# Preparing two dense weight units instead of one beside the experts, and a weight ring of six buffers instead of eight

## The chip, the cores and the metric

The kernel runs on one core of one Trainium2 chip. The metric is device time in microseconds (us) of one execution, as the median of several runs. The engines are named as in the profile: PE multiplies matrices (PEld is its weight load), DVE and ACT are the vector and the scalar engine, POOL is GpSimd, SP only issues DMA transfers.

## The reference, cut to what matters

```
attn_out = banded attention(q, k, v)               # 2 x 8 heads, 576 tokens, window 64
x = attn_out as (1152, 512)
logits = x @ w_gate;  expert = argmax(logits)      # 8 experts
h = np.maximum(einsum('ecd,edf->ecf', disp, w1), 0.0)   # w1: 8 x 512 x 1024, float32
y = einsum('ecf,efd->ecd', h, w2)                  # w2: 8 x 1024 x 512, float32
out[i] = gate_w[i] * y[expert of i, place of i]
h = out @ w_in                                     # dense layer, 512 x 2048, float64 weights
g = h * np.clip(h + 3.0, 0.0, 6.0) / 6.0
return (g @ w_out).astype(np.float32)              # 2048 x 512, float64 weights
```

## The kernel before, in words

The first 75 us are attention and routing. After them come the experts and then the dense layer, and this case is about the weights of these two parts.

**Units and pieces.** The weights are cut into 40 *units* of 256 hidden columns: units 0 to 31 are the eight experts' four quarters each, units 32 to 39 are the dense layer's. A unit has two halves (0: the up-projection, 1: the down-projection), and a half two *pieces* of 128x512 numbers, so a unit has pieces 0 to 3. Every matrix product is done in three passes on a pair of tiles, a rounded part and a remainder (`PASSES`), so before PE can use a piece, it must be *split*: a copy on ACT (L253, the rounded part) and a subtraction on DVE (L258, the remainder), into a tile called `wt`. The experts of two small slots skip the split and multiply from the raw tile.

**Dense pieces cost more.** Their weights arrive as 64-bit numbers and are *converted* first: two instructions on ACT (L201, L204) and four on DVE (L208, L212, L217, L224), in `conv64`. The conversion writes back into the raw tile; for one dense unit it writes into four tiles of its own, `first_w0` to `first_w3`, where the converted piece waits unsplit.

**Buffers.** Raw tiles come from a ring of 8 buffers (`rawp`, `r_raw`); the split halves from a ring of `2 * NWT` = 8 buffers (`wp`, `r_wt`), taken in the order of the units.

**Steps.** PE's work is a list of 84 steps written out in `ORDER` and `GROUPS`: steps 0 to 43 are the experts (three teams, of 16, 12 and 16 steps), steps 44 to 51 the first 640 tokens against dense units 32 to 35 (two steps to a unit), 52 to 67 the other 512 tokens against units 32 to 39, then the rest. Step 20 is the first that uses unit 15; step 44 is the first of the dense part. In a step PE makes the up-projection, in a later one the down-projection of the same slice.

**The planner.** Loads, conversions and splits are *jobs*, each with a due number, sorted by it. While the program is written, an estimate of each engine's clock is kept (`est`); after each group of matmuls `fill` issues the jobs that the estimate has room for, and `need` forces those without which the next step can't run. So the order of instructions on ACT, DVE and SP's queue is settled when the program is built, and each engine then keeps to it. A load gets its place in the raw ring from a count (`raw_at`), the split half its place from `wt_at`.

**The unit that is prepared early.** For unit 32 (`dense0`) the table `FIRST_AT = (5, 9, 14, 20)` says beside which unit each of its four pieces is loaded and converted, into `first_w`. Its splits, and all work on units 33 to 39, have due numbers near their own unit's, that is at the end of the experts and in the dense part.

Of the kernel before, what the change touches and what calls it, by code (L numbers as in the profile page):

```python
# [10 lines left out]
F32R = mybir.dt.float32r  # L11
# [12 lines left out]
def tile_kernel(ctx, tc, q, k, v, w_gate, w1, w2, w_in, w_out, out, cap):  # L24
# [159 lines left out]
    def conv64(u, i, dst=None):  # L184

        box = {}

        def load():
            box["raw"] = raw = rawp.tile([128, 2 * HW], F32, name="raw").bitcast(U32)
            if i < 2:  # L190
                src = w_in32[256 * i : 256 * i + 256, 2 * FU * u : 2 * FU * u + 2 * FU]
                nc.sync.dma_start(raw.rearrange("p (c f) -> p c f", c=2), src.rearrange("(c p) f -> p c f", p=128))
            else:
                r0 = FU * u + 128 * (i - 2)
                nc.sync.dma_start(raw, w_out32[r0 : r0 + 128, :])
            w = raw.rearrange("p (n t) -> p n t", t=2)
            box["lo"], box["hi"] = w[:, :, 0], w[:, :, 1]

        def c_abs():
            box["c"] = cv.tile([128, HW], U32, name="c64")  # L200
            nc.scalar.activation(box["c"].bitcast(F32), box["hi"].bitcast(F32), AF.Abs)  # L201

        def c_round():
            nc.scalar.activation(box["lo"], box["lo"], AF.Copy, scale=2.0 ** -29)  # L204

        def c_clamp():
            c = box["c"].bitcast(F32)
            nc.vector.tensor_scalar(out=c, in0=c, scalar1=TINY, scalar2=HUGE, op0=ALU.max, op1=ALU.min)  # L208

        def c_shift():  # L210
            c = box["c"]
            nc.vector.tensor_scalar(  # L212
                out=c, in0=c, scalar1=0x07FFFFFF, scalar2=3, op0=ALU.bitwise_and, op1=ALU.logical_shift_left
            )

        def a_join():
            nc.vector.scalar_tensor_tensor(  # L217
                out=box["c"], in0=box["hi"], scalar=0xC0000000, in1=box["c"],
                op0=ALU.bitwise_and, op1=ALU.bitwise_or,
            )  # L220

        def t_add():
            out = box["lo"] if dst is None else dst.bitcast(U32)
            nc.vector.tensor_tensor(out=out, in0=box["c"], in1=box["lo"], op=ALU.add)  # L224

        return box, (load, c_abs, c_round, c_clamp, c_shift, a_join, t_add)

    NC64 = 2
# [5 lines left out]
    HALF = UW // 2  # L234
# [12 lines left out]
    def split_ops(w, r, i):  # L247
        n = HALF // 2
        hi, lo = w[:, 0, n * i : n * i + n], w[:, 1, n * i : n * i + n]

        def high(e):
            if e == "A":
                nc.scalar.copy(hi, r)  # L253
            else:
                V.tensor_copy(hi, r)

        def low():
            V.tensor_tensor(out=lo, in0=r, in1=hi.bitcast(F32), op=ALU.subtract)  # L258

        return high, low  # L260
# [28 lines left out]
    key, rank = (rt.tile([128, E], F32, name=n) for n in ("key", "rank"))  # L289
# [720 lines left out]

    NWT = 4
    NRAW = 8
    FIRST_AT = (5, 9, 14, 20)
    NPC = 4
    EOFF = (mybir.EngineType.Activation, mybir.EngineType.DVE)
    NDS = DFF // 128
# [3 lines left out]
    LATE, BESIDE = 10, 2  # L1020

    rawp = ctx.enter_context(tc.tile_pool(name="rawp", bufs=NRAW))
    wp = ctx.enter_context(tc.tile_pool(name="wp", bufs=2 * NWT))
    wk_ctx = ExitStack()
    wk = wk_ctx.enter_context(tc.tile_pool(name="wk", bufs=2))

# [3 lines left out]
    units, steps, unit_of = [], [], {}  # L1030
# [10 lines left out]
    for n, (small, b) in enumerate(TEAMS):  # L1041
        at_ = dict.fromkeys("abw", 0)
# [22 lines left out]
    est = dict.fromkeys(("PE", "A", "V", "P", "D"), 0.0)  # L1065
# [18 lines left out]
            self.rel.append(None)  # L1084
            return len(self.rel) - 1

    r_raw, r_wt, r_ct = Ring(NRAW), Ring(2 * NWT), Ring(NC64)

    def whole(m):

        kind, s, _ = units[m]
        return kind == "e" and SCAP[s] == 64

    wt_at, raw_at = {}, {}
    dense0 = unit_of["d", 0, 0]
    for m in range(len(units)):
        if m != dense0:
            for n in range(2 if units[m][0] == "e" else NPC):
                raw_at[m, n] = len(raw_at)
            for i in range(NPC):  # L1100
                if FIRST_AT[i] == m:
                    raw_at[dense0, i] = len(raw_at)
        for h in range(2):
            if not whole(m):
                wt_at[m, h] = len(wt_at)
    raw_t, raw_ready, wt, half_ready, pieces = {}, {}, {}, {}, {}
    e_of = {}
# [6 lines left out]
    def load_job(m, h):  # L1114
        _, s, u = units[m]

        def gate():
            return r_raw.free(raw_at[m, h])

        def run(e, fin):  # L1120
            take_raw(m, h)
            if u == 0:
                e_of[s] = expert(s)
            weights_in(raw_t[m, h], e_of[s], u, h)
            raw_ready[m, 2 * h] = raw_ready[m, 2 * h + 1] = fin + 3.5
            if whole(m):
                half_ready[m, h] = fin + 3.5
            return fin

        return [({"D": 1.46}, gate, run)]  # L1130

    def conv_job(m, i):
        u = units[m][2]
        ix = {}
        first = m == dense0
        b, (load, c_abs, c_round, *mid, t_add) = conv64(u, i, first_w[i] if first else None)

        def run_load(e, fin):
            r_raw.take()
            load()  # L1140
            raw_t[m, i] = first_w[i] if first else b["lo"].bitcast(F32)
            return fin + 3.5

        def run_abs(e, fin):
            ix["ct"] = r_ct.take()
            c_abs()
            return fin

        def plain(fn):
            def run(e, fin):  # L1150
                fn()
                return fin + 0.13

            return run

        def run_add(e, fin):
            t_add()
            r_ct.rel[ix["ct"]] = fin
            if first:
                r_raw.rel[raw_at[m, i]] = fin  # L1160
            raw_ready[m, i] = fin + 0.2
            return fin + 0.2

        now = lambda: 0.0
        ops = [({"D": 1.46}, lambda: r_raw.free(raw_at[m, i]), run_load), ({"A": 0.6}, r_ct.free, run_abs)]
        ops.append(({"A": 0.57}, now, plain(c_round)))
        ops += [({"V": c}, now, plain(fn)) for c, fn in zip((0.34, 0.34, 0.61), mid)]
        ops.append(({"V": 0.61}, now, run_add))
        return ops

    def split_job(m, i):
        h = i // 2
        box = {}

        def gate():
            r = raw_ready.get((m, i))
            w = 0.0 if (m, h) in wt else r_wt.free(wt_at[m, h])
            return None if r is None or w is None else max(r, w)

        def run_high(e, fin):  # L1180
            if (m, h) not in wt:
                r_wt.take()
                wt[m, h] = wp.tile([128, 2, HALF], F32R, name="wt")
            n = HALF // 2
            r = raw_t[m, h][:, n * (i % 2) : n * (i % 2) + n] if units[m][0] == "e" else raw_t[m, i]
            high, box["low"] = split_ops(wt[m, h], r, i % 2)
            high(e)
            return fin + 0.2

        def run_low(e, fin):  # L1190
            box["low"]()
            pieces[m, h] = pieces.get((m, h), []) + [fin]
            if units[m][0] == "d" and m != dense0:
                r_raw.rel[raw_at[m, i]] = fin
            if len(pieces[m, h]) == 2:
                half_ready[m, h] = max(pieces[m, h])
                if units[m][0] == "e":
                    r_raw.rel[raw_at[m, h]] = half_ready[m, h]
            return fin

        return [({"A": 0.56}, gate, run_high), ({"V": 0.62}, lambda: 0.0, run_low)]

    def add_job(due, unit, ops):
        jobs.append([due, unit, ops, 0.0])

    for m, (kind, s, u) in enumerate(units):
        for i in range(NPC):
            if not whole(m):
                add_job(m + 0.1 * i, m, split_job(m, i))
            if m == dense0:  # L1210
                add_job(FIRST_AT[i] + 1, FIRST_AT[i], conv_job(m, i))
            elif kind == "d":
                add_job(m - AHEAD[1] + 0.1 * i, m, conv_job(m, i))
        if kind == "e":
            for h in range(2):
                add_job(m - AHEAD[0] + 0.1 * h, m, load_job(m, h))
# [32 lines left out]
    def used(m, h):  # L1249
        uses[m, h] -= 1  # L1250
        if not uses[m, h]:
            if whole(m):
                r_raw.rel[raw_at[m, h]] = est["PE"]
            else:
                r_wt.rel[wt_at[m, h]] = est["PE"]

    def gather_rows(a, tag, n=128):
        t = wk.tile([128, DM], F32, name=tag, bufs=3 if tag == "xg" else 1)[0:n]
# [133 lines left out]
    def ts_stage(acc, xt, u, w, last, off, ready, k=None, t0=0):  # L1392
# [4 lines left out]
        if k is not None:  # L1397
            used(k, 0)
# [563 lines left out]
```

## Time and profile before

| | us |
|---|---|
| median of three runs | 428.42 (427.77 to 429.06) |
| the profiled execution | 428.49 |
| its span, first to last instruction | 426.8 |
| PE busy | 403.8 (95%) |
| DVE busy | 290.3 (68%) |
| ACT busy | 242.3 (57%) |

The mean granted clock of TensorE is 0.997 of full speed. A group of equal instructions in a row of the timeline shows its start, its length and its count; the length of a group of matmuls reaches a little past the start of the next, because they are pipelined. What ended the engine's idle time before it stands in brackets, with the length of that idle time.

### The profile page before, as it was taken

Reading aid. Unit: us, or ns where it says so; the run is one execution under the profiler, and the core shown is the slowest. Engines: PE = TensorE matmul, PEld = TensorE weight load, DVE = VectorE, ACT = ScalarE, POOL = GpSimd, SP = SyncE. Lnnn points to the kernel's source line nnn. Section 1 sums busy time; section 2 is a strip of 40 time slices with the busy share of each in tenths; the row PEclk is TensorE's granted clock in tenths of the full one; section 3 lists DMA queues with packets and bytes.
Section 4 is the critical chain, followed back from the end, with each engine's and each line's share of the span. In section 5 each row is a group of like instructions: output and inputs, shape, how many; then the busy total and the mean of one; then the engine's idle time right before and its main releaser. Section 6 shows DMA issues by size and latency. Waiting matters only on the chain.

```text
span 426.8 us, 8494 instructions
## 1 busy us (share of the span) xinstructions
PE 403.8 (95%) x3055; PEld 344.1 (81%) x3055; DVE 290.3 (68%) x801; ACT 242.3 (57%) x526; POOL 50.6 (12%) x108
## 2 busy tenths in 40 slices
PE   7999788899999899999998999999999999999992
PEld 4887664598899899988887899888888888898981
DVE  2888966665889999646889999948896222323430
ACT  4787772655579978345877866548583222422330
POOL 8633404210011001000000000000000000200111
PEclk9999999999999999999999999999999999999998
DMA  9998766997899898759803253233400000110101
GB/s 172 206 225 194 257 240 220 353 356 236 287 320 320 258 375 251 249 191 307 278 8 100 99 192 109 97 98 99 162 38 0 2 0 2 49 49 2 50 27 55
DMA packets 67058, 69.69 MB, mean 163 GB/s; under 512 B 30816, under 2 KB 49248, under 8 KB 67008
## 3 DMA queue, kind: packets, MB, share of 16 engines
q1 hardware_dynamic: 65424, 63.99, 49.0%
q0 software_dynamic: 1584, 5.08, 3.3%
q8 instruction: 26, 0.43, 0.4%
q14 instruction: 24, 0.20, 0.2%
HBM read 64.34 MB, written 4.72 MB: 162 GB/s over the span
## 4 chain that ended last, share of the span: by engine, by line
PE 70%; DVE 16%; DMA 4%; ACT 3%; issue 3%; SPq 1%; POOL 0%; POOLq 0%; ACTq 0%; DVEq 0%
PE banks L239 58%; DVE wt L258 5%; PE banks L1445 2%; PE banks L496 2%; PE banks L614 2%; PE banks L1470 2%; DMA c<-x_dram,sidx 1%; DVE neg L573 1%; PE banks L596 1%; DMA v_sb<-in_v_dram 1%; DVE raw L224 1%; DVE c L217 1%; PE banks L560 1%; SPq L464 1%; ACT wt L253 1%
## 5 line engine op out<-in xcount | busy, mean ns | idle before, releaser
L239 PE MATMUL banks<-x,wt 128*128 128x320 f32 (+3 forms) x576 | 107.9, 337 | 3.0 <-DVE wt L258 2.5
L239 PEld LDWEIGHTS banks<-x,wt 128*128 128x128 f32 x576 | 94.3, 188 | 14.0 <-DVE wt L258 3.9
L239 PE MATMUL banks<-wt,g 128*128 128x512 f32 x384 | 92.8, 390 | 0.0
L258 DVE TENSOR_TENSOR wt<-raw,wt 128x512 fp32r<-128x512 f32 x124 | 80.1, 687 | 14.6 <-ACT wt L253 14.4
L239 PEld LDWEIGHTS banks<-wt,g 128*128 128x128 f32 x384 | 71.6, 188 | 14.2
L253 ACT CAST wt<-raw 128x512 fp32r<-128x512 f32 x124 | 73.0, 631 | 7.8 <-PE banks L239 5.9
L1534 DVE SCALAR_TENSOR_TENSOR gf<-r,banks 128x320 f32<-128x320 f32 (+3 forms) x48 | 26.5, 552 | 53.5 <-ACT r L1531 53.4
L1531 ACT ACTIVATE r<-banks,c_three 128x320 f32<-128x320 f32 (+3 forms) x48 | 27.9, 582 | 59.7 <-PE banks L239 59.6
L239 PE MATMUL banks<-xT,wt 128*128 128x256 f32 (+2 forms) x288 | 38.7, 283 | 1.7 <-DVE wt L258 1.7
L239 PEld LDWEIGHTS banks<-xT,wt 128*128 128x128 f32 x288 | 35.0, 191 | 3.6 <-DVE wt L258 2.1
L239 PE MATMUL banks<-h,wt 128*128 128x256 f32 (+2 forms) x288 | 37.0, 279 | 0.0
L239 PEld LDWEIGHTS banks<-h,wt 128*128 128x128 f32 x288 | 34.6, 191 | 0.5 <-issue 0.5
L1537 ACT CAST g<-gf 128x320 fp32r<-128x320 f32 (+2 forms) x40 | 21.5, 537 | 17.7 <-DVE gf L1534 17.5
L1540 DVE TENSOR_TENSOR g<-gf,g 128x320 fp32r<-128x320 f32 (+2 forms) x40 | 23.3, 583 | 10.0 <-ACT g L1537 9.4
L1577 POOL DMA_INDIRECT out_dram<-raw,cidx x4 | 3.9, 981 | 210.8 <-DVE raw L1571 203.2
L201 ACT ACTIVATE c<-raw 128x512 f32<-128x512 f32 x32 | 21.5, 673 | 11.0 <-DVE raw L224 8.9
L217 DVE SCALAR_TENSOR_TENSOR c<-raw,c 128x512 uint32<-128x512 uint32 x32 | 22.0, 689 | 0.7
L586 ACT ACTIVATE pe<-neg,nmx 128x128 f32<-128x128 f32 x72 | 22.3, 391 | 0.1
L573 DVE CUSTOM_DVE_ANT_0 neg<-banks,tmask 128x128 f32<-128x128 f32 x72 | 16.2, 285 | 8.8 <-PE banks L560 8.8
L791 POOL DMA_INDIRECT xg<-x_dram,sidx x10 | 12.7, 1271 | 79.6 <-PE banks L1281 70.1
L204 ACT ACTIVATE raw<-raw 128x512 uint32<-128x512 uint32 x32 | 21.7, 677 | 0.0
L239 PE MATMUL banks<-wt,xT 128*128 128x256 f32 x144 | 20.6, 290 | 0.3 <-DVE wt L258 0.2
(285 smaller groups left out, 553.3 us busy)
## 6 DMA issues: line engine op xcount, KB each, us to landing
raw<-in_moe_w_dram SPq DMA_DIRECT2D x64, 512.0 KB, 6.1
raw<-in_moe_w_in_dram SPq DMA_DIRECT2D x16, 512.0 KB, 4.7
raw<-in_moe_w_out_dram SPq DMA_DIRECT2D x16, 512.0 KB, 4.8
early<-in_moe_w_dram SPq DMA_DIRECT2D x8, 512.0 KB, 7.8
x_dram<-xt SPq DMA_DIRECT2D x9, 256.0 KB, 3.0
q_sb<-in_q_dram SPq DMA_DIRECT2D x8, 256.0 KB, 4.7
k_sb<-in_k_dram SPq DMA_DIRECT2D x8, 256.0 KB, 4.6
v_sb<-in_v_dram SPq DMA_DIRECT2D x8, 256.0 KB, 4.8
```

The lines of the kernel that those rows point to most:

```text
L201: nc.scalar.activation(box["c"].bitcast(F32), box["hi"].bitcast(F32), AF.Abs)
L204: nc.scalar.activation(box["lo"], box["lo"], AF.Copy, scale=2.0 ** -29)
L217: nc.vector.scalar_tensor_tensor(out=box["c"], in0=box["hi"], scalar=0xC0000000, in1=box["c"], op0=ALU.bitwise_and, op1=ALU.bitwise_or,)
L239: nc.tensor.matmul(out, l, r, start=(start and n == 0), stop=(stop and n == len(pairs) - 1))
L253: nc.scalar.copy(hi, r)
L258: V.tensor_tensor(out=lo, in0=r, in1=hi.bitcast(F32), op=ALU.subtract)
L573: V.tensor_tensor_reduce(out=neg[:, hp, :], in0=box["sp", g][:, hp, :], in1=tmask[:, first, :], scale=-1.0, scalar=3.0e38, op0=ALU.add, op ...
L586: nc.scalar.activation(pe[:, hp, :], neg[:, hp, :], AF.Exp, bias=nmx[:, hp : hp + 1], scale=-1.0)
L1531: nc.scalar.activation(r, ph, AF.Relu, bias=c_three)
L1534: V.scalar_tensor_tensor(out=gf, in0=r, scalar=6.0, in1=ph, op0=ALU.min, op1=ALU.mult)
L1537: nc.scalar.copy(hi, gf)
L1540: V.tensor_tensor(out=lo, in0=gf, in1=hi.bitcast(F32), op=ALU.subtract)
```

## The change: what it does

It makes three edits.

- Unit 32 is now prepared whole beside the experts. Its pieces are loaded and converted beside units 1, 1, 4 and 7, converted in place in the raw tile, and split one unit number later, into two buffers of their own (`wt_fixed`). After unit 32's last use, unit 36 gets these two buffers.
- Unit 33 takes the place that unit 32 had: its pieces are loaded and converted beside units 9, 18, 19 and 21 (`SECOND_AT`), into `first_w`, and split when its turn comes.
- The ring of split halves has six buffers, not eight, for all units but 32 and 36. The raw ring keeps its eight.

```diff
     NRAW = 8
-    FIRST_AT = (5, 9, 14, 20)
+    FIRST_AT = (1, 1, 4, 7)
+    SECOND_AT = (9, 18, 19, 21)
...
-    wp = ctx.enter_context(tc.tile_pool(name="wp", bufs=2 * NWT))
+    wp = ctx.enter_context(tc.tile_pool(name="wp", bufs=2 * NWT - 2))
...
-    r_raw, r_wt, r_ct = Ring(NRAW), Ring(2 * NWT), Ring(NC64)
+    r_raw, r_wt, r_ct = Ring(NRAW), Ring(2 * NWT - 2), Ring(NC64)
...
+    early_at = {(dense0 + n, i): at_[i] for n, at_ in enumerate((FIRST_AT, SECOND_AT)) for i in range(NPC)}
+    fixed = {}
     for m in range(len(units)):
-        if m != dense0:
+        if m not in (dense0, dense0 + 1):
             for n in range(2 if units[m][0] == "e" else NPC):
                 raw_at[m, n] = len(raw_at)
-            for i in range(NPC):
-                if FIRST_AT[i] == m:
-                    raw_at[dense0, i] = len(raw_at)
+            for key, n in early_at.items():
+                if n == m:
+                    raw_at[key] = len(raw_at)
         for h in range(2):
-            if not whole(m):
+            if m in (dense0, dense0 + NWT):
+                fixed[m, h] = 0.0 if m == dense0 else None
+            elif not whole(m):
                 wt_at[m, h] = len(wt_at)
...
-        first = m == dense0
+        first = m == dense0 + 1
...
-            w = 0.0 if (m, h) in wt else r_wt.free(wt_at[m, h])
+            w = 0.0 if (m, h) in wt else fixed[m, h] if (m, h) in fixed else r_wt.free(wt_at[m, h])
...
-                r_wt.take()
-                wt[m, h] = wp.tile([128, 2, HALF], F32R, name="wt")
+                if (m, h) in fixed:
+                    wt[m, h] = wp.tile([128, 2, HALF], F32R, name="wt_fixed", bufs=2)
+                else:
+                    r_wt.take()
+                    wt[m, h] = wp.tile([128, 2, HALF], F32R, name="wt")
...
-            if not whole(m):
+            if m == dense0:
+                add_job(early_at[m, i] + 2, early_at[m, i], split_job(m, i))
+            elif not whole(m):
                 add_job(m + 0.1 * i, m, split_job(m, i))
-            if m == dense0:
-                add_job(FIRST_AT[i] + 1, FIRST_AT[i], conv_job(m, i))
+            if (m, i) in early_at:
+                add_job(early_at[m, i] + 1, early_at[m, i], conv_job(m, i))
...
-            else:
+            elif (m, h) not in fixed:
                 r_wt.rel[wt_at[m, h]] = est["PE"]
+            elif m == dense0:
+                fixed[m + NWT, h] = est["PE"]
```

The kernel after is twelve lines longer, so that from L1100 on its lines have higher numbers: L1341, L1363, L1534, L1540, L1752 and L1756 before are L1353, L1375, L1546, L1552, L1764 and L1768 after. L258 is the same in both.

Three places show what moves. The first is DVE's queue around step 20, in the second team. Before (`wt_2330` is a half of unit 14, `wt_2377` and `wt_2402` the halves of unit 15, `c64_2381` and `first_w2` the third piece of unit 32):

```order
L1341 SCALAR_TENSOR_TENSOR h_2362<-banks_82,h_2362 128x224
L1752 TENSOR_TENSOR cmp_112<-rse_113,top_f_86 128x64
L258 TENSOR_TENSOR wt_2330<-raw_2218,wt_2330 128x512 x2
L258 TENSOR_TENSOR wt_2377<-raw_2222,wt_2377 128x512
L208 TENSOR_SCALAR c64_2381<-c64_2381 128x512
L212 TENSOR_SCALAR c64_2381<-c64_2381 128x512
L1756 TENSOR_REDUCE top_f_86<-cmp_112 128x8
L217 SCALAR_TENSOR_TENSOR c64_2381<-raw_2220,c64_2381 128x512
L224 ISA first_w2_103<-raw_2220,c64_2381 128x1024
L258 TENSOR_TENSOR wt_2377<-raw_2222,wt_2377 128x512
L258 TENSOR_TENSOR wt_2402<-raw_2224,wt_2402 128x512 x2
```

After (`wt_2396` is a half of unit 14, `wt_2414` and `wt_2435` the halves of unit 15, `wt_2438` a half of unit 16):

```order
L258 TENSOR_TENSOR wt_2396<-raw_2255,wt_2396 128x512
L1353 SCALAR_TENSOR_TENSOR h_2399<-banks_82,h_2399 128x224
L1764 TENSOR_TENSOR cmp_112<-rse_113,top_f_86 128x64
L258 TENSOR_TENSOR wt_2396<-raw_2255,wt_2396 128x512
L258 TENSOR_TENSOR wt_2414<-raw_2257,wt_2414 128x512 x2
L1768 TENSOR_REDUCE top_f_86<-cmp_112 128x8
L258 TENSOR_TENSOR wt_2435<-raw_2259,wt_2435 128x512 x2
L258 TENSOR_TENSOR wt_2438<-raw_2261,wt_2438 128x512 x2
```

The conversion that stood between the two pieces of unit 15's first half is gone from this place; the two pieces follow each other.

The second place is DVE's queue in the first two dense steps. Before, the first half of the second dense unit, unit 33 (`wt_3509`), is split from raw tiles after four conversions (`raw_3297`, `raw_3299` and `raw_3301` are pieces 1 to 3 of unit 33, `raw_3303` is piece 0 of unit 34). Here is the end of that stretch:

```order
L217 SCALAR_TENSOR_TENSOR c64_3499<-raw_3303,c64_3499 128x512
L1540 TENSOR_TENSOR g_3538<-gf_3575,g_3538 128x320
L224 ISA raw_3303<-raw_3303,c64_3499 128x512x2
L217 SCALAR_TENSOR_TENSOR c64_3531<-raw_3369,c64_3531 128x512
L258 TENSOR_TENSOR wt_3509<-raw_3202,wt_3509 128x512
L258 TENSOR_TENSOR wt_3509<-raw_3297,wt_3509 128x512
```

After, the same half (`wt_3404`) is split from `first_w` (its piece 0 already in step 43), and the conversions around it belong to units 34 (`raw_3347`) and 35 (`c64_3570`):

```order
L1552 TENSOR_TENSOR g_3526<-gf_3544,g_3526 128x320
L1546 SCALAR_TENSOR_TENSOR gf_3566<-r6_3565,banks_82 128x320
L212 TENSOR_SCALAR c64_3518<-c64_3518 128x512
L217 SCALAR_TENSOR_TENSOR c64_3518<-raw_3347,c64_3518 128x512
L1552 TENSOR_TENSOR g_3526<-gf_3566,g_3526 128x320
L1546 SCALAR_TENSOR_TENSOR gf_3590<-r6_3589,banks_82 128x320
L208 TENSOR_SCALAR c64_3570<-c64_3570 128x512
L224 ISA raw_3347<-raw_3347,c64_3518 128x512x2
L1552 TENSOR_TENSOR g_3576<-gf_3590,g_3576 128x320
L1546 SCALAR_TENSOR_TENSOR gf_3612<-r6_3611,banks_82 128x320
L212 TENSOR_SCALAR c64_3570<-c64_3570 128x512
L258 TENSOR_TENSOR wt_3404<-first_w1_102,wt_3404 128x512
```

Between the last L1375 and the first of these rows stand one each of L212, L217, L1546, L208 and L224. At the start of step 46 the queue has come to unit 35's conversions, where it was at unit 34's before.

The third place is SP's queue of loads at the start of the experts. Before, the loads of units 0 to 5 follow each other, 12 of 512 KB, and then the first dense piece. After, two dense pieces stand between unit 1's second half and unit 2's first:

```order
L269 DMA raw_1496<-in_moe_w2_dram 128x2x512
L192 DMA raw_1525<-in_moe2_w_in_dram 128x2x512
L192 DMA raw_1527<-in_moe2_w_in_dram 128x2x512
L1008 TENSOR_LOAD eofI2_1448
L1008 ISA x2
L266 ISA
L266 DMA raw_1529<-in_moe_w1_dram 128x4x256
```

Each load of units 2, 3 and 4 stands two places later, and the third dense piece comes ahead of unit 5.

## Rows read from the trace of the kernel before

**Rows 1.** PE's waits of the whole span: total us, times, longest.

```profile
PE banks L239 <- DVE wt L258: 4.4, 6, 1.7
```

**Rows 2.** Windows: length; busy us of PE, PEld, DVE, ACT, POOL; clock; DMA share; GB/s.

```profile
76.00:104.00 28.00, 27.34 (x198) 22.17 (x195) 16.60 (x39) 14.80 (x35) 4.33 (x3) 1.00 0.97 318
104.00:137.00 33.00, 32.43 (x269) 28.95 (x268) 28.60 (x70) 24.40 (x55) 3.84 (x3) 1.00 0.92 303
137.00:172.00 35.00, 33.42 (x269) 31.74 (x269) 34.73 (x77) 28.05 (x60) 1.29 (x1) 1.00 0.91 295
172.00:215.50 43.50, 43.50 (x380) 38.13 (x378) 27.30 (x60) 25.48 (x59) 0.00 (x0) 1.00 0.75 246
215.50:272.30 56.80, 53.82 (x298) 47.92 (x298) 55.33 (x114) 40.53 (x78) 0.00 (x0) 1.00 0.35 112
```

**Rows 3.** PE's timeline, steps 18 and 20: start, length, instruction, count, idle before.

```profile
135.96 1.58 PE L239 MATMUL banks<-xT,wt 128*128 128x224 f32 x12
...
141.53 0.83 PE L239 MATMUL banks<-xT,wt 128*128 128x224 f32 x6
143.82 0.93 PE L239 MATMUL banks<-xT,wt 128*128 128x224 f32 x6 [1.45 <-DVE wt L258]
```

**Rows 4.** DVE's timeline just ahead of step 20's second half.

```profile
140.72 0.42 DVE L208 TENSOR_SCALAR c<-c 128x512 f32<-128x512 f32 x1
...
141.65 0.68 DVE L217 SCALAR_TENSOR_TENSOR c<-raw,c 128x512 uint32<-128x512 uint32 x1
142.47 0.69 DVE L224 CUSTOM_DVE_ANT_0 first_w<-raw,c 128x1024 uint16<-128x1024 uint16 x1
143.08 1.28 DVE L258 TENSOR_TENSOR wt<-raw,wt 128x512 fp32r<-128x512 f32 x2
```

**Rows 5.** PE's timeline, dense steps 44 to 48.

```profile
215.53 0.56 PE L239 MATMUL banks<-x,wt 128*128 128x320 f32 x2
216.50 0.85 PE L239 MATMUL banks<-x,wt 128*128 128x320 f32 x4 [0.40 <-ACT x L1361]
...
223.98 3.59 PE L239 MATMUL banks<-wt,g 128*128 128x512 f32 x15
227.41 0.74 PE L239 MATMUL banks<-x,wt 128*128 128x320 f32 x4
...
233.15 3.59 PE L239 MATMUL banks<-wt,g 128*128 128x512 f32 x15
236.58 3.68 PE L239 MATMUL banks<-x,wt 128*128 128x320 f32 x24
240.09 3.59 PE L239 MATMUL banks<-wt,g 128*128 128x512 f32 x15
...
248.05 2.23 PE L239 MATMUL banks<-wt,g 128*128 128x512 f32 x9
```

**Rows 6.** DVE's groups by form, 215.5 to 272.3: busy us, mean ns, idle before.

```profile
L1540 DVE TENSOR_TENSOR g<-gf,g 128x320 fp32r<-128x320 f32 x16 | 7.8, 488 | 0.0
L1534 DVE SCALAR_TENSOR_TENSOR gf<-r,banks 128x320 f32<-128x320 f32 x16 | 7.7, 481 | 0.0
```

**Rows 7.** DVE's timeline, the last copy of the experts' output.

```profile
216.48 0.59 DVE L1363 TENSOR_TENSOR x<-banks,x 128x416 f32 x1 [0.37 <-ACT x L1361]
```

**Rows 8.** SP's queue: the sixth expert load (unit 2's second half).

```profile
72.44 0.38 SPq L269 DMA_DIRECT2D raw<-in_moe_w_dram  x1
```

**Rows 9.** The raw tiles in 72.3 to 72.6: that load's time to landing.

```profile
DMA to landing us min/median/max: 9.1/9.1/9.1
```

**Rows 10.** ACT's timeline, the copies ahead of the first expert step.

```profile
82.06 0.58 ACT L1284 CAST xT<-banks 128x512 fp32r<-128x512 f32 x1
84.12 0.59 ACT L452 COPY c<-banks 128x512 f32<-128x512 f32 x1 [1.48 <-PE banks L239]
```

**Rows 11.** PE's timeline, the up-projection of step 4 (unit 3).

```profile
93.55 1.60 PE L239 MATMUL banks<-wt,xT 128*128 128x256 f32 x12
```

**Rows 12.** The page's costliest groups: the split's copy on ACT.

```profile
L253 ACT CAST wt<-raw 128x512 fp32r<-128x512 f32 x124 | 73.0, 631 | 7.8 <-PE banks L239 5.9
```

More of the change, by code (lines that the diff above doesn't have):

```diff
@@ L1192, in run_low @@
             pieces[m, h] = pieces.get((m, h), []) + [fin]
-            if units[m][0] == "d" and m != dense0:
+            if units[m][0] == "d" and m != dense0 + 1:
                 r_raw.rel[raw_at[m, i]] = fin
```

## The prediction

> **What bounds the kernel now.** I read the shares of the page first: PE is busy 95% of a span at full clock, so the kernel is bound by PE's own matmuls, and only about 23 us in which PE does nothing, or is kept from its pace, can be won without taking matmuls away. Then I read who keeps PE waiting, over the whole span. The reader should see one row [rows 1]: six waits, 4.4 us together, for the subtraction on DVE that ends a split. A wait in this view ends where a matmul starts, so the lost pace around it is not in it. I therefore went on to windows by stage [rows 2] and to PE's timeline. The windows show why DVE is late where it is: from 137 to 172 it is busy 34.73 of 35 us, and in the first part of the dense layer, 215.5 to 272.3, 55.33 of 56.8. Between them, and ahead of them, it has room: 11.4 us idle in 76 to 104, 4.4 in 104 to 137, 16.2 in 172 to 215.5. PE, on its part, has 43.50 of 43.50 in 172 to 215.5: nothing can be won there, only lost.
>
> **Place one, step 20.** The same 12 matmuls take 1.58 us in step 18. In step 20 they start at 141.53, stop after six for 1.45, and end at 143.82 + 0.93 = 144.75 [rows 3]: 3.22, so 1.64 lost. DVE's rows say why [rows 4]: between the two splits of that half stand four instructions of a dense conversion (0.42, a second one like it, 0.68, 0.69), and the split that PE wants starts at 143.08. After the change no conversion stands between them. ACT's copies of these tiles don't move later, so the second piece is ready some two microseconds sooner, about 141, before PE wants it (141.53 plus six matmuls, 0.8). The window has as many conversions as before (two, by my count of the order), but they stand further on, beside steps 23 to 26. **Gain 1.64.**
>
> **Place two, steps 44 to 48.** In an unhindered step the up-projection takes 240.09 − 236.58 = 3.51, and the down-projection 236.58 − 233.15 = 3.43 [rows 5]. Against these:
>
> - 215.53 to 223.98 is 8.45 for two up-projections (7.02): 1.43 lost, in it the wait for ACT's last copy of the experts' output.
> - 227.41 to 233.15 is 5.74 for one up-projection: 2.23 lost.
> - 240.09 to 248.05 is 7.96 for a down- and an up-projection (6.94): 1.02 lost.
>
> Together 4.68. Of it, the wait for the copy stays, since the change doesn't touch it: the two matmuls ahead of it take 0.29 at the pace of 3.51/24 each, and the next starts 0.97 after them, so 0.68. The rest, **4.00**, I count as gained, because DVE has less to do: four conversions and four splits of a dense unit are done before this window. A conversion is 2 × 0.42 + 0.68 + 0.69 = 2.2 us on DVE, a split 0.6 (143.08 to the end of two is 1.28), so 4 × 2.8 = 11.3 us, and DVE's 55.33 becomes about 44.
>
> That is a mean; what counts is when the halves are ready. Step 46 wants unit 33's first half. In the order, DVE issues ahead of its end, from the last copy at 216.48 [rows 7], 5 light (0.42) and 5 heavy (0.69) instructions of conversions and splits and 4 + 3 of the activation (0.481, 0.488) [rows 6]: 8.9 us, ready at 226.0 by durations. PE, with its losses gone, wants it at 215.53 + 0.68 + 7.02 + 3.43 = 226.66. Step 48 wants unit 34's first half: 6 light, 12 heavy and 4 + 4 ahead of it, 14.6 more, so 240.6; PE wants it at 226.66 + 2 × (3.51 + 3.43) = 240.54. Both are just in time. Rows that follow each other directly start some 0.08 closer than their durations say (142.47 to 143.08 is 0.61 for one of 0.69), which gives a microsecond back in either place, so I take no loss here.
>
> **What it costs earlier.** The four conversions and four splits don't vanish. By my count from the order, three conversions and the four splits (9.1 us of DVE) move into 76 to 137, where DVE is idle 15.8. The fourth conversion goes into 172 to 215.5, and four splits of the experts slip there from the window ahead: together 4.6 us, with 16.2 idle. ACT gets 0.63 for each split [rows 12], and for each conversion two passes over as large a tile, about 1.3 by the same row; it is busy 14.80 of 28 and 24.40 of 33. On average this cover holds. If it were gone, the whole 11.3 us would be at stake, so each early step has to be looked at:
>
> - *The queue of loads.* Two loads of 512 KB now stand ahead of unit 2's. The DMA engines are at 0.97 of their time in 76 to 104 at 318 GB/s, so each later load lands 1.65 us later for each dense piece ahead. The load that stood sixth was issued at 72.44 and landed 9.1 later [rows 8, 9], at 81.5. This is now where the second dense piece lands.
> - *ACT.* The conversion's first instruction on these pieces stands in order ahead of the copies for the experts at 82.06 and 84.12 [rows 10]. At 81.5 it is in time for the second, with 2.6 to spare. On the first dense piece (fifth load, a load earlier, about 80) it is 2 ahead of the copy at 82.06.
> - *Unit 3.* Its second piece is split on DVE at about 92.6 by counting its load two places back (3.3 us) and the queue; PE takes it at 93.55 [rows 11]. This margin of 0.9 is the smallest that I find before step 20.
> - *Steps 23 to 32.* Two conversions of unit 33 now stand there among the splits, and a third follows, where DVE was full before. I find margins of 0.5 to 1 us there.
>
> I take 0.6 for two new short waits in these places, each like the mean of the short ones before: of the six waits of 4.4 [rows 1], take away the longest (1.7) and the 1.45 at step 20; 1.25 is left over four, 0.3 each.
>
> **The ring of six.** A split half can start when the half six places before it has been used. Counted over the order, the buffer is free 8 to 10 us before PE wants what goes into it, and a split of a half takes 1.3 on each engine, so this costs PE nothing. ACT's waits for PE at the copy (5.9 us now [rows 12]) may grow. The Trainium skill speaks against this edit: "Perfetto Trace Analysis", section Identifying Performance Opportunities, reads the same gap repeated on the engine that should be full as a sign that there isn't enough SBUF for the next tile. The trace before shows no such repeated gap in 172 to 215.5, where PE is full; no run so far has six buffers.
>
> **The sum.** 428.49 − 1.64 − 4.00 + 0.6 = 423.45. The profiled run is 0.07 above the median of the three, so I forecast **423.4**.
>
> **The rivals.**
>
> - *Smaller gain.* The just-in-time places (steps 23 to 32, 46, 48) each lose what the bounds allow: at 46 and 48 a conversion in the way is 2.2. For it speaks that DVE has no slack in 137 to 172 and margins at 46 and 48 are under 0.7; against it that work only moved out of the dense window. One such wait of 2.2 and some short ones: about 426.
> - *No change: the ring of six binds.* If a half can only be split after PE has let go of the buffer, and DVE, in its fixed order, is held at that split, the halves come late by a little in each unit. Some 0.5 us at ten units from 137 to 205 is 5, and the gain is gone: 428. Against it: the 8 to 10 us by which a buffer is free ahead.
> - *Slower: the dense pieces at the head of ACT's queue.* ACT keeps to its order. If the second dense piece lands later than 84.1 instead of 81.5, the copy for the experts, and behind it the split copies of units 0 to 3, wait, and with the saturated DMA of 0.92 to 0.97 share nothing catches up until step 20: each unit from 2 to 15 comes up to two loads, 3.3 us, late, and a third dense piece ahead of unit 5 makes it 5. It decides against the change when PE loses more than 5.6 + 1.3 = 7 us by it; two such delays that PE can't make good (5 + 3.3, without the 0.6) give 428.4 − 5.6 + 8.3 = 431. Against it: a second load issued at the same time doesn't hold back the first by more than its own 1.65, and DVE's and ACT's idle time in 76 to 104 shows slack in front of PE. The Trainium skill has the rule on which this rests: "PSUM — Partial Sum Buffer", section Engine vs sequencer instructions, calls the queues of ScalarE and VectorE strict first in, first out. The timelines before agree: each row of DVE in [rows 4] starts after the one before it, the split at 143.08 behind a conversion that it doesn't need.
> - *Bigger gain.* The short waits of the experts' first part go too, and none comes: 421.9.
>
> **How the numbers follow.** Chances: forecast 0.64, smaller gain 0.16, no change 0.11, slower 0.07, bigger gain 0.02. A measurement of this kernel tells about 0.3%, 1.3 us, from no change. Faster is then 0.64 + 0.16 + 0.02 = 0.82, same 0.11, slower 0.07. The likeliest case by itself runs from 422.0 (hardly a new wait) to 424.9 (the unknown waits at twice their price, and 0.9 more at steps 46 and 48). The range for 8 in 10 goes on to the smaller gain and stops short of the other two: 421.6 to 427.0.
>
> **What would show it right or wrong.** Right: PE's 12 matmuls of step 20 in one run of 1.6 us; steps 44 to 47 at 3.5 and 3.4 a projection behind the 0.68; DVE busy about 44 in the first 53 us of the dense part and more in 76 to 104; waits of PE for the split under 1.5 us in all. Wrong: a wait at steps 3 to 5 behind a late raw tile or a copy on ACT at 82 to 85; idle time of DVE or ACT with PE as releaser at many splits (the ring); new waits at steps 23 to 32 or at 46 and 48. The prediction falls if step 20's gap shows up again a few steps on, since then a conversion there is a cost that moves and is not hidden.

## The result, and the profile after

The kernel after takes 425.24 us (median of 5 runs, 423.79 to 425.64), the kernel before 429.06 beside it (5 runs, 427.77 to 429.94). The ratio is 0.990, with an interval of 0.988 to 0.992, so the change saves 4.3 us (3.4 to 5.2), where 5.0 were forecast. The profiled execution took 425.50, with a span of 423.8.

PE's waits over the whole span, from 0.8 us up and those of L239:

```profile
PE banks L239 <- ACT first_w L452: 1.7, 2, 1.3
PE banks L1390 <- ACT c L452: 1.5, 1, 1.5
PE banks L653 <- DVE warm L650: 1.4, 1, 1.4
PE banks L1293 <- DVE c L1285: 1.1, 1, 1.1
PE banks L845 <- ACT first_w L834: 0.8, 2, 0.5
PE banks L970 <- DVE A1t L965: 0.8, 1, 0.8
...
PE banks L239 <- ACT x L1373: 0.4, 1, 0.4
...
PE banks L239 <- DVE wt L258: 0.2, 1, 0.2
```

The wait for the split, 4.4 us in six pieces before [rows 1], is down to one of 0.2. At the top stand two waits for copies on ACT (L452). The second, L1390 for `c`, is not among the waits of before. The windows, with the columns of [rows 2]:

```profile
76.00:104.00 28.00, 24.92 (x178) 19.78 (x179) 22.01 (x49) 17.60 (x39) 3.30 (x3) 1.00 0.88 294
104.00:137.00 33.00, 32.56 (x262) 28.67 (x261) 29.09 (x72) 24.41 (x54) 4.56 (x3) 1.00 1.00 338
137.00:172.00 35.00, 35.00 (x287) 33.74 (x286) 33.63 (x77) 28.45 (x61) 1.79 (x1) 1.00 0.90 285
172.00:215.50 43.50, 43.50 (x379) 38.23 (x380) 33.00 (x71) 27.77 (x64) 0.00 (x0) 1.00 0.89 290
215.50:272.30 56.80, 56.40 (x320) 51.30 (x320) 48.85 (x100) 35.59 (x69) 0.00 (x0) 1.00 0.21 75
```

PE is busy 1.6 us longer in 137 to 172 and 2.6 in the last window, and 2.4 less in the first; the pace that it loses around a wait is not in these numbers. The two gains are the two places of the prediction. Step 20 on PE's timeline (start, length, instruction, count, idle before), and the dense steps 44 to 48 and 52:

```profile
144.63 1.51 PE L239 MATMUL banks<-xT,wt 128*128 128x224 f32 x12
...
217.50 7.01 PE L239 MATMUL banks<-x,wt_fixed 128*128 128x320 f32 x46 [0.40 <-ACT x L1373]
224.34 3.59 PE L239 MATMUL banks<-wt_fixed,g 128*128 128x512 f32 x15
227.77 3.68 PE L239 MATMUL banks<-x,wt 128*128 128x320 f32 x24
...
245.16 3.59 PE L239 MATMUL banks<-wt,g 128*128 128x512 f32 x15
...
269.41 2.88 PE L239 MATMUL banks<-x,wt_fixed 128*128 128x512 f32 x12
```

Step 20's 12 matmuls run through in 1.51 (3.22 before [rows 3]). From the first matmul behind the copy to the down-projection behind step 48's up-projection it is 245.16 − 217.50 = 27.66; before it was 248.05 − 216.50 = 31.55 [rows 5]. That is 3.89 gained.

The loss in the first window is told by ACT and DVE around 84 to 88. First ACT's timeline, then DVE's, then PE's:

```profile
84.22 0.69 ACT L204 ACTIVATE raw<-raw 128x512 uint32<-128x512 uint32 x1
84.79 0.68 ACT L201 ACTIVATE c<-raw 128x512 f32<-128x512 f32 x1
87.60 0.58 ACT L452 COPY c<-banks 128x512 f32<-128x512 f32 x1 [2.14 <-DVE raw L224]
88.08 0.68 ACT L204 ACTIVATE raw<-raw 128x512 uint32<-128x512 uint32 x1
```

```profile
86.83 0.68 DVE L224 CUSTOM_DVE_ANT_0 raw<-raw,c 128x1024 uint16<-128x1024 uint16 x1
```

```profile
88.24 0.66 PE L1390 MATMUL banks<-ident,c 128*128 128x128 f32 x4 [1.49 <-ACT c L452]
```

The last row holds the transposes of the early expert's output, which stand at step 0 and are called step 0's transposes below. ACT's copy of that output needs nothing of a dense conversion, yet it waits 2.14 us for the last instruction of one (L224, ending at 87.51), and PE waits 1.49 for the copy. Before, the same copy waited for PE alone and started at 84.12 [rows 10]. The code suggests the cause: the copy's target and the conversion's scratch tile have the same name in one pool of two.

```
cv = ctx.enter_context(tc.tile_pool(name="cv", bufs=2))
box["yE"] = t = cv.tile([128, HW], U32, name="c64").bitcast(F32)   # the copy's target
box["c"] = cv.tile([128, HW], U32, name="c64")                     # c_abs of a conversion
```

In the order, two conversions of unit 32 now take their tiles ahead of the copy, so the copy has the third, and has to wait until the first conversion is through. E1 and E6 test this. The load of the second dense piece, issued at 71.1, landed 10.4 later, at 81.5, where the forecast had it:

```profile
DMA to landing us min/median/max: 10.4/10.4/10.4
```

### The profile page after: what moved, and what is told of

It is laid out like the page before. It is cut to its first block, busy times and chain, and to the rows that moved or that the text cites. A ratio compares the mean times of both kernels' runs of the same rounds, so it can differ in the third digit from the quotient of the medians.

```text
span 423.8 us, 8491 instructions
## 1 busy us (share of the span) xinstructions
PE 403.3 (95%) x3055; PEld 345.1 (81%) x3055; DVE 290.4 (69%) x801; ACT 241.7 (57%) x526; POOL 50.8 (12%) x108
## 4 chain that ended last, share of the span: by engine, by line
PE 84%; DVE 6%; DMA 3%; ACT 2%; issue 2%; SPq 1%; POOL 0%; POOLq 0%; ACTq 0%; DVEq 0%
PE banks L239 71%; PE banks L614 2%; PE banks L1457 2%; PE banks L496 2%; PE banks L1482 2%; DMA c<-x_dram,sidx 2%; PE banks L596 1%; DMA v_sb<-in_v_dram 1%; DVE neg L573 1%; SPq L464 1%; PE banks L560 1%; PE banks L1293 1%; DVE wt L258 1%; PE banks L1419 1%; PE banks L526 1%
## 5 line engine op out<-in xcount | busy, mean ns | idle before, releaser
L239 PE MATMUL banks<-x,wt 128*128 128x320 f32 (+3 forms) x432 | 79.8, 336 | 0.0
L258 DVE TENSOR_TENSOR wt<-raw,wt 128x512 fp32r<-128x512 f32 x116 | 74.4, 682 | 4.0 <-ACT wt L253 3.7
L239 PEld LDWEIGHTS banks<-x,wt 128*128 128x128 f32 x432 | 70.8, 188 | 7.1
L253 ACT CAST wt<-raw 128x512 fp32r<-128x512 f32 x116 | 67.5, 629 | 6.4 <-PE banks L239 3.2
L239 PE MATMUL banks<-wt,g 128*128 128x512 f32 x288 | 69.6, 390 | 0.0
L1546 DVE SCALAR_TENSOR_TENSOR gf<-r,banks 128x320 f32<-128x320 f32 (+3 forms) x48 | 26.5, 553 | 60.3 <-ACT r L1543 60.1
L239 PEld LDWEIGHTS banks<-wt,g 128*128 128x128 f32 x288 | 53.7, 188 | 10.6
L239 PE MATMUL banks<-xT,wt 128*128 128x256 f32 (+2 forms) x288 | 38.6, 283 | 0.1
L239 PE MATMUL banks<-h,wt 128*128 128x256 f32 (+2 forms) x288 | 37.0, 279 | 0.0
L239 PEld LDWEIGHTS banks<-xT,wt 128*128 128x128 f32 x288 | 35.0, 191 | 1.9 <-ACT wt L253 0.4
L239 PEld LDWEIGHTS banks<-h,wt 128*128 128x128 f32 x288 | 34.6, 191 | 0.5 <-issue 0.5
L1552 DVE TENSOR_TENSOR g<-gf,g 128x320 fp32r<-128x320 f32 (+2 forms) x40 | 23.3, 583 | 10.1 <-ACT g L1549 9.4
L239 PE MATMUL banks<-x,wt_fixed 128*128 128x320 f32 (+3 forms) x144 | 26.8, 337 | 0.4 <-ACT x L1373 0.4
L239 PEld LDWEIGHTS banks<-x,wt_fixed 128*128 128x128 f32 x144 | 23.5, 188 | 3.0 <-ACT x L1373 0.7
L239 PE MATMUL banks<-wt_fixed,g 128*128 128x512 f32 x96 | 23.2, 390 | 0.0
L217 DVE SCALAR_TENSOR_TENSOR c<-raw,c 128x512 uint32<-128x512 uint32 x32 | 22.0, 688 | 0.6
```

The source lines that it names most:

```text
L217: nc.vector.scalar_tensor_tensor(out=box["c"], in0=box["hi"], scalar=0xC0000000, in1=box["c"], op0=ALU.bitwise_and, op1=ALU.bitwise_or,)
L239: nc.tensor.matmul(out, l, r, start=(start and n == 0), stop=(stop and n == len(pairs) - 1))
L1546: V.scalar_tensor_tensor(out=gf, in0=r, scalar=6.0, in1=ph, op0=ALU.min, op1=ALU.mult)
L1552: V.tensor_tensor(out=lo, in0=gf, in1=hi.bitcast(F32), op=ALU.subtract)
```

## The experiments

**E1. The copy gets a tile of its own.**

```diff
-            box["yE"] = t = cv.tile([128, HW], U32, name="c64").bitcast(F32)
+            box["yE"] = t = first_w[3]
```

> The kernel after, with the early expert's output copied into a tile of its own (first_w3, unused until unit 33's fourth piece) instead of a third scratch tile of a pool of two. Theory (a tile of the pool has to come free): ACT's copy no longer waits 2.14 us for the end of the first conversion, PE's wait of 1.49 before step 0's transposes goes, and the kernel ends 1.5 us (up to 1.7) sooner than the kernel after, about 423.6; the wait of 1.27 at 80.6 stays. Rival (ACT's order: the conversion's instructions ahead of the copy are what costs): the copy is as late as before, 0 to 0.3 us gained, about 425.

422.83 us (422.04 to 425.47, 6 runs), before 429.40 on that chip: 0.9853 (0.9824 to 0.9882). PE's wait before step 0's transposes is gone, and the rows of E6 below show the copy. Since the kernel after was not run beside it, E5 and E6 repeat the pair on one chip.

**E2. Unit 32's first two pieces later.**

```diff
-    FIRST_AT = (1, 1, 4, 7)
+    FIRST_AT = (3, 3, 4, 7)
```

> The kernel after, with unit 32's first two pieces beside unit 3 instead of unit 1 (FIRST_AT 3, 3, 4, 7), so that their loads stand behind unit 3's and their conversions behind the early expert's output. Theory (all that is lost is lost at the start, to the two loads beside unit 1's and to the scratch tile): both waits at 80.6 and 88.2 go, 2.6 us sooner than the kernel after, about 422.6, if no split of units 4 to 6 comes late; one such wait would cost up to 1. Rival (the loss is one of work, DVE and ACT being too full in 76 to 104): the same 2.6 us are lost at steps 4 to 8 instead, about 425.

423.40 (422.85 to 423.44, 5 runs): 0.9859 (0.9837 to 0.9881). Both waits at the start are gone. PE's timeline has two others in their place:

```profile
97.51 0.98 PE L239 MATMUL banks<-xT,wt 128*128 128x256 f32 x6 [0.47 <-DVE wt L258]
...
109.87 0.98 PE L239 MATMUL banks<-xT,wt 128*128 128x256 f32 x6 [0.82 <-DVE wt L258]
```

So the rival has a part: with the conversions later, short waits come at steps 5 and 9, which want units 4 and 7 (step 9 had one of 0.23 before). The cost at the start was not one of too much work, since most of it did not come back. Since E2 moves the loads, the conversions and the order of tiles together, it doesn't tell which of them mattered; E1 does.

**E3. A conversion put back into step 20.**

```diff
-    SECOND_AT = (9, 18, 19, 21)
+    SECOND_AT = (9, 14, 19, 21)
```

> The kernel after, with unit 33's second piece beside unit 14 instead of 18, which puts the conversion back on DVE between the two splits of unit 15's first half. Theory (order on DVE at step 20): PE waits there again about 1.4 us, the kernel is 1.4 to 1.7 slower than the kernel after, about 426.8. Rival (step 20's gap came from something else, for instance the raw tile's landing or ACT): no wait there, about 425.2.

426.10 (425.35 to 428.00, 6 runs): 0.9928 (0.9903 to 0.9953), where the kernel after has 0.990. PE's timeline at step 20:

```profile
144.04 0.83 PE L239 MATMUL banks<-xT,wt 128*128 128x224 f32 x6
146.07 0.93 PE L239 MATMUL banks<-xT,wt 128*128 128x224 f32 x6 [1.19 <-DVE wt L258]
146.83 1.51 PE L239 MATMUL banks<-h,wt 128*128 128x224 f32 x12
```

The stall is back, a little shorter than before: the next group starts 146.83 − 144.04 = 2.79 after, against 1.34 in the kernel after (144.63 to 145.97), so 1.45 lost. The ratios differ by 0.0028, 1.2 us, but their intervals overlap; the place is shown, the size is taken from the trace.

**E4. The kernel before, with the conversion behind unit 15's splits.**

```diff
-    FIRST_AT = (5, 9, 14, 20)
+    FIRST_AT = (5, 9, 16, 20)
```

> The kernel before, with the third piece of unit 32 beside unit 16 instead of 14, so that its conversion stands behind all of unit 15's splits; nothing else is changed. Theory: step 20's wait of 1.45 goes and the kernel is 1.6 us faster than the kernel before, about 427 where before is 428.6; the dense part is as before. Rival (a conversion only moves its wait): a wait of about the same size at steps 21 to 24, no gain.

427.93 (427.12 to 429.43, 12 runs), before 429.40: 0.9965 (0.9950 to 0.9979), so 1.5 us faster (0.9 to 2.1). Step 20 is clean, and the dense waits stand as before, 0.38, 1.66 and 0.44. At steps 21 to 24 there is no wait for a split, but ahead of step 27 PE waits 0.95 for another thing, the scaling of gathered rows on DVE (L1273):

```profile
143.28 1.51 PE L239 MATMUL banks<-xT,wt 128*128 128x224 f32 x12
...
164.53 0.66 PE L1281 MATMUL banks<-ident,xg 128*128 128x128 f32 x4 [0.95 <-DVE xg L1273]
164.94 1.58 PE L239 MATMUL banks<-xT,wt 128*128 128x224 f32 x12
```

From step 20 to step 27 it is 164.94 − 143.28 = 21.66 here and 22.54 in the kernel before (141.53 to 164.07), so in this profile about half of the gain at step 20 is kept. DVE is busy 25.03 of the 25.10 us from 138.9 to 164.0, so in this profile part of the wait moved on to another job of a full DVE. The profiled execution was the longest of the twelve; by the median the gain is there, and what the other runs lost ahead of step 27 is not known.

**E5 and E6. The kernel after and E1's kernel again, on one chip.**

> The kernel after, unchanged, on the chip of the next three. Its span held two waits at the start that the kernel before had not or had shorter: 1.27 at 80.6 (before 0.34) and 1.49 at 88.2. Theory: the second belongs to the program and is there again within 0.1; the first hangs on when unit 1's load lands, which differs from execution to execution (it was 0.55 and 0.88 in two kernels with the same loads, 1.32 in one with the loads of before), and may be anything from 0.3 to 1.3. Rival: the first belongs to the program too (the two dense loads beside unit 1's) and is about 1.2 again. Time about 1 % under the kernel before either way.

> The kernel after with the early expert's output in a tile of its own, once more, beside the kernel after on one chip. Theory (scratch tile): 1.5 us, at most 2, under the kernel after, with no wait before step 0's transposes. Rival (the difference seen between chips was the chip's): less than 0.7 under it.

The kernel after: 425.46 (424.07 to 426.83, 6 runs), 0.9906 (0.9880 to 0.9932). With the tile of its own: 423.00 (422.39 to 424.35, 6 runs), 0.9856 (0.9834 to 0.9879). The medians are 2.5 us apart, more than the 2 that were expected at most. In E5 PE's timeline has both waits:

```profile
80.50 1.98 PE L239 MATMUL banks<-early,first_w 128*128 128x512 f32 x4 [1.21 <-ACT first_w L452]
88.12 0.66 PE L1390 MATMUL banks<-ident,c 128*128 128x128 f32 x4 [1.49 <-ACT c L452]
```

In E6 neither is there:

```profile
79.27 1.98 PE L239 MATMUL banks<-early,first_w 128*128 128x512 f32 x4
...
85.24 0.60 PE L1390 MATMUL banks<-ident,first_w 128*128 128x128 f32 x4
```

ACT's timeline of E6 shows the copy (its target is now `first_w`) directly behind the second conversion's first instruction, and the rest of that conversion behind it:

```profile
83.42 0.70 ACT L201 ACTIVATE c<-raw 128x512 f32<-128x512 f32 x1
84.01 0.59 ACT L452 COPY first_w<-banks 128x512 f32<-128x512 f32 x1
84.50 0.70 ACT L204 ACTIVATE raw<-raw 128x512 uint32<-128x512 uint32 x1
```

ACT issues the same instructions in the same order as in the kernel after, with the conversion ahead of the copy, and the copy doesn't wait. That rules out the order on ACT as what cost 1.49; it was the tile. The Trainium skill's "PSUM — Partial Sum Buffer", section Engine vs sequencer instructions, on which a rival of the prediction leaned, is right about the strict order: in the kernel after ACT stood idle for 2.14, and the second conversion's L204, which needs nothing of the copy, stood behind it. But the order alone costs a copy here only what runs ahead of it.

The wait at 80 to 81 is another matter. It was 1.27 and 1.21 in two profiles of the kernel after, 0.55 in E1 and not there in E6, which are one program; 0.88 in E3 and 0.73 in E8, which have the same early loads. In kernels with the loads of the old table it was 0.34 (before), 1.32 (E4), 0.37 (E9), and not there in E7. ACT's rows behind it say what it waits for; in E4, which has the loads of before:

```profile
79.40 1.14 ACT L253 CAST wt<-raw 128x512 fp32r<-128x512 f32 x2 [1.26 <-DMA raw<-in_moe_w_dram]
```

Unit 1's second half landed late there too, 8.9 us after its issue against 7.5 in the kernel before. So this wait differs from execution to execution, with either table, and that the two dense loads add to it is not shown.

**E7. The ring of six alone.** The old table, unit 33 at its old place, unit 32's splits held back to step 41; the two fixed buffers and the ring of six stay.

```diff
+        if i == 41:
+            fixed[dense0, 0] = fixed[dense0, 1] = 0.0
```

> The kernel before with the ring of six and two fixed buffers for units 32 and 36 alone: the old table, unit 33 at its old place, unit 32's splits held back to the end of the experts. In the order only ACT and DVE at steps 17 to 32 differ from before (splits up to one step later). My reason (a buffer is free 8 to 10 us ahead): the same time as the kernel before within 0.3 %, no new wait for the split in 137 to 215, step 20's and the dense part's waits as before. Rival (the ring binds): about 0.5 us at each of some ten units, 2 to 5 us slower.

428.26 (427.29 to 431.39, 12 runs), before 429.11: 0.9985 (0.9967 to 1.0002). The ring costs nothing that can be told. PE's timeline has the waits of before at step 20 and in the dense part, with none between step 20 and step 44:

```profile
143.05 0.93 PE L239 MATMUL banks<-xT,wt 128*128 128x224 f32 x6 [1.20 <-DVE wt L258]
...
228.65 3.51 PE L239 MATMUL banks<-x,wt 128*128 128x320 f32 x20 [1.68 <-DVE wt L258]
```

**E8. Only unit 32 early.** The kernel after without `SECOND_AT`.

```diff
-    early_at = {(dense0 + n, i): at_[i] for n, at_ in enumerate((FIRST_AT, SECOND_AT)) for i in range(NPC)}
+    early_at = {(dense0 + n, i): at_[i] for n, at_ in enumerate((FIRST_AT,)) for i in range(NPC)}
...
-        first = m == dense0 + 1
+        first = False
```

> The kernel after without the second early unit: unit 32 whole beside the experts, unit 33 at its old place, everything else as after. Theory (the dense gain is DVE's load in steps 44 to 48): step 20 is clean (no conversion near it), four splits fewer than before in the dense part but four conversions (2.2 us each) more than after, so PE waits again for unit 33's and 34's halves; of the 4.0 us I expect 1 to 2.5 kept, by the four splits of 0.6. About 2 us above the kernel after. Rival (it is the splits and the fixed buffers that give the dense gain, not the conversions): no wait in steps 44 to 48, about the same as the kernel after.

426.52 (425.36 to 427.26, 6 runs): 0.9930 (0.9907 to 0.9953), some 1.0 us above E5 on the same chip, though the intervals of the two overlap. PE's timeline:

```profile
216.83 7.01 PE L239 MATMUL banks<-x,wt_fixed 128*128 128x320 f32 x46 [0.40 <-ACT x L1373]
...
227.10 4.03 PE L239 MATMUL banks<-x,wt 128*128 128x320 f32 x24
...
241.33 4.34 PE L239 MATMUL banks<-x,wt 128*128 128x320 f32 x24
...
255.87 4.06 PE L239 MATMUL banks<-x,wt 128*128 128x320 f32 x24
...
270.14 2.88 PE L239 MATMUL banks<-x,wt_fixed 128*128 128x512 f32 x12
```

No row behind the first names a wait, but three of the up-projections take 4.03, 4.34 and 4.06 where a clean one shows 3.68. The view of PE's own waits has nothing on them; that of PE's weight loads has it, from 215 to 272 (total, times, longest):

```profile
PEld banks L239 <- DVE wt L258: 1.3, 4, 0.3
PEld banks L239 <- ACT x L1373: 0.7, 1, 0.7
```

The dense steps 44 to 51, from the first matmul behind the copy to step 52, take 270.14 − 216.83 = 53.31. In the kernel after it is 51.91, and in the kernel before, where step 52 starts at 272.32, it was 55.82. So unit 32 alone brings 2.5 of the 3.9, the upper end of what I expected, and unit 33's conversions the other 1.4.

**E9. Only the early split.** The table of before, with the fixed buffers and the ring of six. Unit 32's pieces are loaded and converted at their old places, and split as soon as ACT and DVE have time: E7's kernel without the two lines that hold the splits back.

> The kernel before with one part of the change: unit 32's pieces loaded and converted at their old places (5, 9, 14, 20), but split as soon as the engines have time, into two fixed buffers, beside a ring of six; unit 33 as before. The kernel with unit 32 whole early and unit 33 late kept 2.5 of the 3.9 us that the dense steps gained. Theory (what counts there is DVE's load, and unit 32's four splits of 0.6 are 2.4 of it): from the start of step 44's second group to the end of step 51 the 55.8 us of before become 53.3, step 20's stall stays, nothing is lost at the start: 2.5 us under the kernel before, about 426.5. Rival (the conversions' earlier place is what gave the 2.5): the dense steps take 55 or more, about 428.5.

425.80 (425.58 to 426.21, 6 runs), before 428.83: 0.9929 (0.9910 to 0.9948), so 3.0 us faster (2.2 to 3.9). PE's timeline:

```profile
144.02 0.93 PE L239 MATMUL banks<-xT,wt 128*128 128x224 f32 x6 [1.54 <-DVE wt L258]
216.32 7.01 PE L239 MATMUL banks<-x,wt_fixed 128*128 128x320 f32 x46 [0.40 <-ACT x L1370]
...
269.62 2.88 PE L239 MATMUL banks<-x,wt_fixed 128*128 128x512 f32 x12
```

Step 20's stall is there, and the dense steps take 53.30, as in E8. Hence four splits moved away give the 2.5, with the conversions left where they were.

## Why the prediction was right, and what it missed

**Step 20 (1.64).** Right in place and size. Taking the conversion out of this place alone gives 1.5 (E4), putting one back brings the stall (E3). In the kernel after PE waits for no split between step 20 and step 44, so the gap does not turn up a few steps on, which was the prediction's own sign of being wrong. E4's profile is a warning: there 0.95 us came back ahead of step 27.

**Steps 44 to 48 (4.00).** Right: 3.89. The two just-in-time halves came in time. The second piece of unit 33's first half, on DVE's timeline, is split 1.1 us before PE wants it at 227.77:

```profile
225.97 0.68 DVE L258 TENSOR_TENSOR wt<-first_w,wt 128x512 fp32r<-128x512 f32 x1
```

The sum by DVE's load was off, though: I said about 44 us busy, and DVE is busy 48.85 in the 53 us from 216.4. In steps 44 to 51 it ran 16 conversions and 15 splits before (counted by L217 and L258), and 14 and 11 after: with room to spare it takes up two conversions of later units that stood behind step 51 before. The gain follows from when the first halves are ready, and not from the busy time that is left. E8 and E9 give it term by term: 2.5 from the four splits of unit 32, 1.4 from unit 33's conversions.

**The ring of six (0).** Right (E7). The sign that "Perfetto Trace Analysis" in the Trainium skill gives for a lack of SBUF, the same gap repeated, doesn't show in E7's trace. What was short of a buffer was another pool, and it showed as one gap, not as a repeated one.

**The 0.6 for two new short waits.** What moved ahead went where the prediction put it: three conversions and the four splits to 76 to 137, one conversion to 172 to 215.5. The 0.6 was wrong in place: neither unit 3 nor steps 23 to 32 wait. The kernel after has a wait of 0.24 at step 8, as before, and no other for a split.

**The step that failed** is the one on ACT: "At 81.5 it is in time for the second, with 2.6 to spare." It asked when the conversion's pieces land and what stands ahead of the copy in ACT's queue, and not into which tile the copy writes. What it asked, it had right: the piece landed at 81.5. The copy at 84.12 in [rows 10] was named as the place; what held it there was the pool of two scratch tiles, for 1.49 us of PE's time plus what its matmuls lost of their pace. Without it the kernel is at 0.9853 and 0.9856 of before (E1, E6), 6.2 to 6.3 us faster, where the forecast's two gains make 5.64. With it the gain is 3.8 by the medians and 4.3 by the ratio. The difference of 2.5 between E5 and E6 holds more than the 1.5 to 1.7 of this wait; the wait for unit 1's load (1.21 in the one profile, none in the other) may be the rest, but only single profiles show it.

**What was luck.** 425.24 lies in the range because the range made room for another loss, a wait of 2.2 at steps 23 to 32, 46 or 48 (the rival at about 426). None of these waits came; the loss that came was the copy's, where the prediction had 2.6 to spare.

**The profiled pair by marks.** Step 0's transposes start 2.90 later than before (88.24, before 85.34). Of this 1.66 is the scratch tile (they start 3.48 behind the 12 matmuls ahead of them, 1.82 before), and 1.24 arises ahead of it, where the load of unit 1 and the first gather differ between executions. From there to step 20 another 0.20 is lost (56.39 for 56.19). At step 20 1.71 come back, by steps 21 to 43 0.39, and 3.91 in steps 44 to 51: 2.90 + 0.20 − 1.71 − 0.39 − 3.91 = −2.91, against 423.8 − 426.8 = −3.0 in the spans.

**A version that beats both** is E1's: the change, with the copy in `first_w3`, 422.83 and 423.00 in two sets of runs, against 425.46 for the kernel after on the second chip.

## What to carry to other kernels

When work is moved ahead of other work, go through what each moved instruction takes from a ring or a pool, and who takes the next piece of it: a shared tile name binds two parts of a program that have no data in common. A wait whose releaser has nothing to do with the waiting instruction's data was the mark of it in this trace. And where a group of matmuls is longer than its equals while no wait is named, look at the waits of the weight loads. On an engine that is full, as DVE is from 137 to 172, a job moved out of one instruction's way can hold back another one further on (E4).

## What the runs showed of the hardware that was not expected

The same load, issued from the same place in the queue (unit 1's second half, 512 KB), landed 7.5 us after its issue in one profile of the old table and 8.9 in another. PE's wait behind this landing was 1.32 us in one profile (E4) and not there in another of the same loads (E7), so a single profile can't tell it from a cost of the change.
